# Windowed attention with a cosine-gated MLP: casts and weights issued earlier, block loads ahead of outputs, MLP units recounted in four blocks

## The chip, the cores and the metric

One core of a Trainium2 chip runs the kernel. The metric is the device time of one execution in microseconds (us), lower is better. Before the change it is 408.87 us, the median of 3 runs (406.36 to 410.55).

## The reference

Eight batches of eight heads, 576 positions of 64 elements. A query sees keys at a distance of at most 32, and eight global positions see and are seen by everything. The attention's output, laid out as 4608 tokens of 512 elements, goes through an MLP with h·cos(h) between its two products.

```python
scores = scale * np.matmul(q, k.transpose(0, 1, 3, 2))
mask = np.abs(pos[:, None] - pos[None, :]) <= window          # 32
mask = mask | is_global[:, None] | is_global[None, :]
attn = softmax(np.where(mask, scores, -1e9))                  # eight global positions
x = np.matmul(attn, v).transpose(0, 2, 1, 3).reshape(4608, 512)
h = x @ w_in                                                  # 512 x 2048
out = (h * np.cos(h)) @ w_out                                 # 2048 x 512
```

## The kernel before

**Work and its tiles.** Heads are taken in pairs (`pr`, 0 to 31), four pairs to a batch; two pairs make a half batch, and one half batch is one block `s` (0 to 15) of the main loop. For a pair, `scores` (L500 to L503) multiplies keys by queries in three groups of windows (`st`), takes the exponential on ScalarE (`e`) and masks on VectorE (`pm`). `values` (L512 to L523) multiplies by the values (`pv`) and normalises on VectorE (`xn`). `turn_x` (L535 to L543) transposes on TensorE (`tx`) and writes the tokens into `xT`, after a batch's last pair with eight small GpSimd copies for the global positions. The MLP runs on tiles `t` of 512 tokens. An in unit (`mlp_in`, L551 to L555) is four matmuls into `ph`, a cosine on ScalarE and a product on VectorE; 16 of them make `g` of one tile. An out unit (`mlp_out`, L565) is four matmuls into `po`; after four of them `po` is copied out (by VectorE and ScalarE in turn) and SP stores it (L574). There are 144 units of each kind.

**Inputs.** For half batches 0 to 3 keys and queries are loaded by GpSimd (`load_qk`), transposed on TensorE (`turned`) and copied by ScalarE and VectorE (`local_k`, `local_q`). Values come by 24 loads on SP (`load_vn`) into `vn32`, are cast by VectorE and ScalarE (`cast_vn`, L343 to L346), and `spread` (L365 to L372) moves them with matmuls into the value tiles `vw` of one pair. From half batch 4 on, `cast_half` has GpSimd's queue cast v, k and q from DRAM to DRAM (`v16`, `k16`, `q16`), and SP then brings them in: `turn_half` (two transposing DMAs into `kT` and `qT`, two buffers each) and `load_values` (into `vw`, four buffers). VectorE copies `kT` and `qT` into `kw` and `qb` (L477, L490).

**The order.** It is written by hand. `FRONT` is a list of steps for the first six pairs: `k1` is `local_k(1)`, `C0` is `cast_vn(0)`, `w0` is `spread(0)`, `s1.0` the first group of scores of pair 1, `p` is `values`, `x` is `turn_x`, `W` loads a quarter of `w_in`, `O` loads `w_out`, `V` is `hold`, `n` is `x_squares`, a checksum on ScalarE, and `I` loads the positions into GpSimd's registers. A `hold` is a GpSimd copy of one element of `vn32`, which keeps what follows in GpSimd's queue until that load has landed. The blocks 2 and 3 have lists of their own, `THIRD` and `FOURTH`; all later ones use `ORDER`. In these `1` is an in unit and `2` an out unit, and the letter behind a step names a pair: `a` and `z` are the block's own two, `c` and `d` the next block's. `G` runs `casts(s)`: a copy that waits for the block's `xn` (the gate), the casts of a later half batch, and in block 4 also six indirect loads of the global rows of batches 4 to 7 (`gather`), which `build_globals(1)` uses at the end of block 5. In units run only for tiles whose tokens are there (`ready`), out units up to the cap `outs_by`. At the end of a block SP is given the loads of the block after next. Blocks 4 and 5 take half batches 4 and 5, which are the fifth and the sixth.

Of the kernel before, what the change touches and what calls it, by code (L numbers as in the profile page):

```python
# [23 lines left out]
G = 8  # L24
# [17 lines left out]

THIRD = "1 1 C2 w4 pa 1 w5 1 xa V3 W3 O pz kc qc 1 1 xz kd qd 1 C3 wc G 1 wd n 1 1"

FOURTH = "sa0 sa1 sa2 sz0 sz1 sz2 pa 1 1 xa pz 1 1 G xz n R 2 1 2 1 2 1 2 1 2 1 2 1 2 1 2 kc qc 1 2 1 2 kd qd 1 2 1 2"

FRONT = ("s0.0 s0.1 s0.2 k1 q1 C0 w0 s1.0 s1.1 s1.2 L2 p0 k2 q2 C1 w1 x0 s2.0 s2.1 s2.2 p1 g4 k3 q3 w2 W1 x1 s3.0 s3.1 s3.2 p2 L3 g5 w3 x2 k4 q4 p3 "
         "g6 g7 I s4.0 s4.1 s4.2 x3 n0 k5 q5 V2 W2 s5.0 s5.1 s5.2")
OK_ALL = float(P * (B * NP * 2 * BP + B))
# [144 lines left out]
def kernel(  # L194
# [462 lines left out]

    def load_w_out(_):
        nc.gpsimd.dma_start(w_out16, moe_w_out.rearrange("(c p) n -> p c n", p=P))
        cast_half(4, "vkq")  # L660

    STEPS = {"s": scores, "p": values, "x": turn_x}
    with tc.manual_schedule():
# [40 lines left out]
        def load_values(pr):  # L704
            load_v(pr)
            load_vg(pr)
# [9 lines left out]
        def globals_kq(pr):  # L716
            globals_k(pr)
            globals_q(pr)

        def casts(s):  # L720

            nc.gpsimd.tensor_copy(gate, xn_of[s][0:1, 1, 0, 0:1])  # L722
            for n in range(4, 2 * B):
                if s == n - 3:
                    cast_half(n, "vkq")
            if s == 4:
                for src, dst in ((k, kg32), (q, qg32), (v, vg32)):
                    gather(src, dst, 1)

        LOCAL = {"k": local_k, "q": local_q}  # L730
        OTHER = LOCAL | {"g": globals_kq, "L": load_qk, "W": load_w_in, "c": lambda s: cast_half(s, "v"), "v": load_values, "n": x_squares,
                 "I": load_idx, "w": spread, "C": cast_vn, "V": hold, "O": load_w_out}
        for step in FRONT.split():
# [9 lines left out]
        for s in range(2, B * NP // 2):  # L743
            outs_by[0] = 16 if s < 5 else 8 * (s - 3)
            for pr in (2 * s + 2, 2 * s + 3):
                if 8 <= pr < B * NP:
                    globals_kq(pr)
            for step in {2: THIRD, 3: FOURTH}.get(s, ORDER).split():
# [6 lines left out]
                elif step == "R":  # L755
                    ready[0] = 2
                elif step == "G":
                    casts(s)
# [6 lines left out]
            if s % 2 == 1:  # L765
                ready[0] = s // 2 + 1 + (s // 2 == B - 1)
            if s < B * NP // 2 - 2:
                turn_half(s + 2)
                load_values(2 * s + 4)
                load_values(2 * s + 5)  # L770
            if s == 5:
# [50 lines left out]
```

## Time and profile before

| what | value |
|---|---|
| median of 3 runs | 408.87 us (406.36 to 410.55) |
| the profiled execution's own time | 405.1 us |
| its span, first to last instruction | 403.4 us |
| mean granted TensorE clock | 0.954 |
| TensorE matmul busy | 348.2 us, 86% |
| VectorE busy | 266.5 us, 66% |
| ScalarE busy | 249.6 us, 62% |
| GpSimd busy | 111.1 us, 28% |

The busy times are of one profiled execution; its span is 1.7 us shorter than its time. A busy share is a mean over stages with different limits, so it is the single blocks that have to be looked at: block 2 runs from 50.30 to 81.34 us, block 3 to 115.72, block 4 to 133.11, block 5 to 146.72, block 6 to 165.84. After block 15, near 315 us, only MLP units are left.

### The profile page before, as it was taken

What the parts mean: (1) busy time and instruction counts of PE and PEld (TensorE: products, weight loads), DVE (VectorE), ACT (ScalarE), POOL (GpSimd) and SP (SyncE); (2) the same over time, 40 slices, a digit from 0 to 9 for tenths busy, and PEclk for the clock granted to TensorE, in tenths of its full rate; (3) what the DMA queues carried; (4) which work ended last, traced back from release to release, by engine and by line L of the source; (5) the groups of instructions that cost most, each with busy time, mean ns of one, the idle gap of its engine ahead of it and who ended that gap; (6) DMA issues with size and microseconds to landing.
All of it is one profiled execution on the core that took longest, in us unless ns stands there. A gap on an engine that the chain in (4) does not pass through costs nothing.

```text
span 403.4 us, 7909 instructions
## 1 busy us (share of the span) xinstructions
PE 348.2 (86%) x2934; PEld 191.7 (48%) x2934; DVE 266.5 (66%) x615; ACT 249.6 (62%) x372; POOL 111.1 (28%) x249
## 2 busy tenths in 40 slices
PE   0499579777998459999999999999999969999993
PEld 0388446543444335555555555555555424444441
DVE  7649457455557857788887888878888445544300
ACT  5567646484458626768777786777867866244300
POOL 6734352306003644442516416141100100000000
PEclk9999579889999859999999999999999999999998
DMA  6996099999339999999999999999980000010111
GB/s 100 198 208 93 4 181 196 158 84 75 57 77 118 178 117 150 187 122 199 106 172 161 141 193 143 177 170 128 160 81 34 26 2 26 26 54 27 54 78 59
DMA packets 175318, 45.55 MB, mean 113 GB/s; under 512 B 163881, under 2 KB 170281, under 8 KB 175081
## 3 DMA queue, kind: packets, MB, share of 16 engines
q1 hardware_dynamic: 111449, 27.41, 50.4%
q0 software_dynamic: 63824, 17.57, 44.1%
q8 instruction: 25, 0.41, 0.4%
q14 instruction: 20, 0.16, 0.2%
HBM read 45.07 MB, written 20.05 MB: 161 GB/s over the span
## 4 chain that ended last, share of the span: by engine, by line
PE 71%; DVE 8%; ACT 7%; DMA 5%; issue 4%; POOL 4%; POOLq 0%; ACTq 0%; DVEq 0%
PE po L565 29%; PE ph L551 26%; PE st L500 5%; PE t L369 4%; DVE g L555 4%; PE pv L512 3%; DMA vg<-in_v_dram,gidx_rows 3%; ACT cos L554 2%; PE tx L535 2%; PE t L365 2%; DMA kn<-in_k_dram 2%; ACT e L502 2%; POOL q L257 1%; ACT qb L487 1%; DVE qb L487 1%
## 5 line engine op out<-in xcount | busy, mean ns | idle before, releaser
L551 PE MATMUL ph<-xT,w_in 128*128 128x512 f16 x576 | 143.8, 385 | 7.0 <-DVE g L555 5.0
L554 ACT ACTIVATE cos<-ph,pio 128x512 f16<-128x512 f32 x144 | 97.2, 686 | 74.7 <-PE ph L551 72.3
L565 PE MATMUL po<-w_out,g 128*128 128x512 f16 x576 | 142.1, 383 | 1.1 <-DVE o L572 1.1
L555 DVE TENSOR_TENSOR g<-cos,ph 128x512 f16<-128x512 f16 x144 | 96.4, 686 | 66.2 <-ACT cos L554 62.8
L551 PEld LDWEIGHTS <-w_in 128*128 128x128 f16 x576 | 54.1, 99 | 69.2 <-issue 12.4
L565 PEld LDWEIGHTS <-g 128*128 128x128 f16 x576 | 55.8, 98 | 65.2 <-issue 3.7
L502 ACT ACTIVATE e<-st 128x512 f16<-128x512 f32 (+1 forms) x96 | 47.7, 563 | 15.4 <-PE st L500 10.0
L503 DVE TENSOR_TENSOR pm<-e,mask 128x512 f16<-128x512 f16 (+1 forms) x96 | 37.3, 404 | 25.3 <-ACT e L502 23.3
L722 POOL COPY gate<-xn 1x1 f16<-1x1 f16 x14 | 2.5, 179 | 162.4 <-DVE xn L523 162.4
L500 PE MATMUL st<-qb,kw 128*128 128x128 f16 x352 | 30.3, 233 | 13.1 <-DVE qb L487 4.9
L500 PEld LDWEIGHTS <-kw 128*128 128x128 f16 x352 | 25.4, 104 | 22.6 <-issue 11.6
L523 DVE TENSOR_TENSOR xn<-pv,r_all 128x768 f16<-128x768 f32 x32 | 30.6, 958 | 1.9
L369 PE MATMUL t<-xT 112*128 112x128 f16 (+1 forms) x168 | 23.0, 255 | 5.7 <-DVE xT L343 5.2
L257 POOL DMA_DIRECT2D q<-in_q_dram x12 | 26.2, 2183 | 0.0
L570 ACT COPY o<-po 128x512 f32<-128x512 f32 x18 | 10.5, 585 | 22.4 <-PE po L565 22.1
L543 POOL COPY xT<-xg 128x4 f16 x64 | 19.7, 308 | 14.8 <-DVE xT L538 11.4
L584 ACT ACTIVATE sq<-xn 128x1536 f16<-128x1536 f16 x16 | 23.6, 1478 | 0.0
L535 PE MATMUL tx<-ident,xn 128*128 128x128 f16 x192 | 17.0, 228 | 6.6 <-DVE xn L523 6.6
L490 DVE COPY qb<-qT 64x616 f16<-64x616 f16 x48 | 22.1, 460 | 0.3
L535 PEld LDWEIGHTS <-xn 128*128 128x128 f16 x192 | 13.4, 102 | 14.7 <-DVE xn L523 9.1
L572 DVE COPY o<-po 128x512 f32<-128x512 f32 x18 | 12.3, 684 | 12.0 <-PE po L565 12.0
L365 PE MATMUL t<-vg,xT 128*128 128x128 f16 x88 | 20.2, 255 | 0.0
(121 smaller groups left out, 342.5 us busy)
## 6 DMA issues: line engine op xcount, KB each, us to landing
out_dram<-o SPq DMA_DIRECT2D x36, 256.0 KB
vw<-v SPq DMA_DIRECT2D x35, 165.0 KB
v<-in_v_dram POOLq DMA_DIRECT2D x12, 288.0 KB, 5.1
k<-in_k_dram POOLq DMA_DIRECT2D x12, 288.0 KB, 8.0
q<-in_q_dram POOLq DMA_DIRECT2D x12, 288.0 KB, 11.8
vn<-in_v_dram SPq DMA_DIRECT2D x20, 112.0 KB
w_in<-in_moe_w_in_dram POOLq DMA_DIRECT2D x4, 512.0 KB, 8.0
w_out<-in_moe_w_out_dram POOLq DMA_DIRECT2D x1, 2048.0 KB, 17.6
```

The source lines that it names most:

```text
L257: nc.gpsimd.dma_start(dst[s].rearrange("t (h d) -> t h d", h=4), dview(src, base, (D, S), (S * D, 4), (1, D)))
L365: nc.tensor.matmul(t[:, j - g0], own[:, pr], vg16[:, 0].rearrange("p h d -> p (h d)"), start=True, stop=False)
L369: nc.tensor.matmul(t[:, j - g0], shift[0:m, a], new[0:m, x, h0 : h0 + 2 * D], start=False, stop=(a, x) == parts[-1])
L500: nc.tensor.matmul(st[:, j], kp[:, g0 + j], view(qp[:, g0 + j], (1, P)), start=True, stop=True)
L502: nc.scalar.activation(e[:, :n], st[:, :n], AF.Exp, scale=scale)
L503: nc.vector.tensor_tensor(view(pm[:, g0], (1, n * P)), view(e, (1, n * P)), view(mask[:, g0], (1, n * P)), ALU.mult)
L523: nc.vector.tensor_tensor(view(xn, (384, 2), (D, 6), (1, D)), view(pv, (512, 2), (65, 6), (1, D)), view(rp, (6, 2), (1, 6), (0, D)), ALU.mult)
L535: nc.tensor.transpose(tx[:, n], xn[:, n], ident16)
L551: nc.tensor.matmul(ph, w_in16[:, j, f * P : (f + 1) * P], xT[:, j, t * TT : (t + 1) * TT], start=(j == 0), stop=(j == NC - 1))
L554: nc.scalar.activation(cos, ph, AF.Sin, bias=pio2)
L555: nc.vector.tensor_tensor(g16[:, f], cos, ph, ALU.mult)
L565: nc.tensor.matmul(po, g16[:, f, s * P : (s + 1) * P], w_out16[:, f], start=(f == 0), stop=(f == NF - 1))
```

## The change

It moves steps and changes counts; apart from the two holds, and from a few table loads that ScalarE needs where cosines and exponentials now alternate, the same instructions run. The holds `V2` and `V3` go. `W2` moves up to behind `W1`; `W3` and `O` move from block 2 and the end of `FRONT` to a place before pair 3's `turn_x`; `O` now issues the cast of half batch 4's values ahead of `w_out`, and the new step `K` issues its keys and queries and all of half batch 5. The casts of half batches 6 and 7 move one block earlier (`G` of blocks 2 and 3), so `G` of block 4 has only the gathers. `C2` moves from block 2 into `FRONT`, `n0` the other way, `C3` from right before `wc` to one unit before it. For block 5 SP's loads (`bring`) are issued inside block 3 (step `T`), ahead of that block's outputs; for block 4 the value loads now stand ahead of the transposes. Units: block 2 keeps 10 in units; block 3 goes from 15 in and 12 out to 6 in and 8 out; block 4 from 7 in and 4 out to 8 and 4; block 5 from none to 8 and 4. At the end of block 5 both kernels have run 32 in units and 16 out units.

```diff
-THIRD = "1 1 C2 w4 pa 1 w5 1 xa V3 W3 O pz kc qc 1 1 xz kd qd 1 C3 wc G 1 wd n 1 1"
+THIRD = "1 1 w4 n0 pa 1 w5 1 xa pz kc qc C3 1 wc 1 xz kd qd 1 wd 1 n 1 1 G"
...
-FOURTH = "sa0 sa1 sa2 sz0 sz1 sz2 pa 1 1 xa pz 1 1 G xz n R 2 1 2 1 2 1 2 1 2 1 2 1 2 1 2 kc qc 1 2 1 2 kd qd 1 2 1 2"
+FOURTH = "sa0 sa1 sa2 sz0 sz1 sz2 pa 1 1 xa pz G 1 1 xz T n R 1 1 2 2 2 2 kc qc 2 2 kd qd 2 2"
...
-FRONT = ("s0.0 s0.1 s0.2 k1 q1 C0 w0 s1.0 s1.1 s1.2 L2 p0 k2 q2 C1 w1 x0 s2.0 s2.1 s2.2 p1 g4 k3 q3 w2 W1 x1 s3.0 s3.1 s3.2 p2 L3 g5 w3 x2 k4 q4 p3 "
-         "g6 g7 I s4.0 s4.1 s4.2 x3 n0 k5 q5 V2 W2 s5.0 s5.1 s5.2")
+FRONT = ("s0.0 s0.1 s0.2 k1 q1 C0 w0 s1.0 s1.1 s1.2 L2 p0 k2 q2 C1 w1 x0 s2.0 s2.1 s2.2 p1 g4 k3 q3 w2 W1 W2 x1 s3.0 s3.1 s3.2 p2 L3 g5 w3 x2 C2 p3 "
+         "g6 g7 I W3 O k4 x3 K q4 s4.0 s4.1 s4.2 k5 q5 s5.0 s5.1 s5.2")
...
     def load_w_out(_):
+        cast_half(4, "v")
         nc.gpsimd.dma_start(w_out16, moe_w_out.rearrange("(c p) n -> p c n", p=P))
-        cast_half(4, "vkq")
+
+    def cast_more(_):
+        cast_half(4, "kq")
+        cast_half(5, "vkq")
...
+        def bring(s):
+
+            if s > 4:
+                turn_half(s)
+            load_values(2 * s)
+            load_values(2 * s + 1)
+            if s == 4:
+                turn_half(s)
...
-            for n in range(4, 2 * B):
-                if s == n - 3:
+            for n in range(6, 2 * B):
+                if s == n - (4 if n < 8 else 3):
                     cast_half(n, "vkq")
...
-            outs_by[0] = 16 if s < 5 else 8 * (s - 3)
+            outs_by[0] = 4 * (s - 1) if s < 5 else 8 * (s - 3)
...
+                elif step == "T":
+                    bring(s + 2)
...
-            if s < B * NP // 2 - 2:
-                turn_half(s + 2)
-                load_values(2 * s + 4)
-                load_values(2 * s + 5)
+            if s != 3 and s < B * NP // 2 - 2:
+                bring(s + 2)
```

On ScalarE the cosine of each in unit stands in a row of L554, so the recount can be read there. From the first cosines of block 3 to the first exponentials of block 4 it was, before:

```order
L554 ACTIVATE cos<-ph,pio_71 128x512 x4
L584 ACTIVATE sq,x_sq<-xn 128x1536
L554 ACTIVATE cos<-ph,pio_71 128x512 x7
L570 COPY o<-po 128x512
L554 ACTIVATE cos<-ph,pio_71 128x512 x4
L502 ACT_TABLE_LOAD
L502 ACTIVATE e<-st 128x512 x2
```

and it is now:

```order
L554 ACTIVATE cos<-ph,pio_71 128x512 x4
L584 ACTIVATE sq,x_sq<-xn 128x1536
L554 ACTIVATE cos<-ph,pio_71 128x512 x2
L570 COPY o<-po 128x512
L502 ACT_TABLE_LOAD
L502 ACTIVATE e<-st 128x512 x2
```

Nine of the fifteen cosines have left block 3, and the copy of an output stands last before the table load.

On VectorE in `FRONT`, around the normalising of pair 3 (`xn`, L523), the two casts of `cast_vn(2)` (L343, L346) come in, and the copy of pair 4's queries (`qb`, L487) goes behind pair 3's `turn_x`. Before:

```order
L538 COPY xT_82<-tx_773 128x616
L487 COPY qb0_99<-t_800 64x11x56
L517 TENSOR_REDUCE dg_841<-pv_292 8x2
L518 RECIPROCAL r_all_119<-pv_292 128x12
L519 RECIPROCAL r_all_119<-dg_841 8x12
L523 TENSOR_TENSOR xn_728<-pv_292,r_all_119 128x768
L503 TENSOR_TENSOR pm_932<-e_938,mask_114 128x512
```

and now:

```order
L538 COPY xT_82<-tx_774 128x616
L343 CAST xT_82<-vn32_112 112x768
L346 CAST xT_82<-vn32_112 16x256
L517 TENSOR_REDUCE dg_808<-pv_292 8x2
L518 RECIPROCAL r_all_119<-pv_292 128x12
L519 RECIPROCAL r_all_119<-dg_808 8x12
L523 TENSOR_TENSOR xn_729<-pv_292,r_all_119 128x768
L537 TENSOR_REDUCE xg_529<-tx_920 128x8
L538 COPY xT_82<-tx_920 128x616
L487 COPY qb0_99<-t_942 64x11x56
```

The scores of pair 4 need that `qb`, so they now follow pair 3's normalising and turning.

On GpSimd at the gate of block 4, ahead of the globals' copies for block 6 (`kw0`, `qb0`), stood before:

```order
L722 COPY gate_113<-xn_1901 1x1
L253 DMA v16_81<-in_v_dram 16x9216
L257 DMA k16_80<-in_k_dram 2304x1x64
L257 DMA q16_79<-in_q_dram 2304x1x64
L293 DMA kg32_104<-in_k_dram,gidx_rows_106 128x64 x2
L293 DMA qg32_103<-in_q_dram,gidx_rows_106 128x64 x2
L293 DMA vg32_105<-in_v_dram,gidx_rows_106 128x64 x2
L454 COPY kw0_95<-kgT_116 128x11x8
```

and now:

```order
L735 COPY gate_113<-xn_1809 1x1
L293 DMA kg32_104<-in_k_dram,gidx_rows_106 128x64 x2
L293 DMA qg32_103<-in_q_dram,gidx_rows_106 128x64 x2
L293 DMA vg32_105<-in_v_dram,gidx_rows_106 128x64 x2
L454 COPY kw0_95<-kgT_116 128x11x8
```

The cast of half batch 7 has gone from in front of the gathers to the gate of block 3.

## Rows read from the trace of the kernel before

**Rows 1.** Windows, blocks 2 to 7: us, busy per engine, clock, DMA share, GB/s
```profile
50.30:81.34 31.04, 25.46 (x291) 17.50 (x290) 17.19 (x40) 17.22 (x27) 10.96 (x15) 0.86 1.51 177
81.34:115.72 34.38, 29.02 (x187) 13.79 (x186) 20.00 (x41) 19.31 (x30) 6.88 (x18) 0.95 0.68 64
115.72:133.11 17.39, 13.60 (x123) 6.94 (x122) 12.60 (x30) 12.71 (x20) 4.94 (x5) 1.00 1.04 129
133.11:146.72 13.61, 5.12 (x81) 3.89 (x81) 10.78 (x28) 6.57 (x14) 5.59 (x9) 0.66 1.52 138
146.72:165.84 19.12, 19.12 (x143) 9.96 (x143) 12.39 (x29) 10.98 (x17) 13.54 (x31) 0.88 1.46 154
165.84:182.75 16.91, 16.91 (x143) 9.06 (x142) 14.54 (x34) 12.92 (x19) 5.47 (x12) 1.00 1.51 152
```
**Rows 2.** Timeline of TensorE, blocks 3 and 4: start, us, operation, [idle <-releaser]
```profile
93.83 1.03 PE L565 MATMUL po<-w_out,g 128*128 128x512 f16 x4
94.70 1.03 PE L551 MATMUL ph<-xT,w_in 128*128 128x512 f16 x4
...
99.60 1.02 PE L551 MATMUL ph<-xT,w_in 128*128 128x512 f16 x4 [1.28 <-POOL xT L543]
...
117.13 2.75 PE L565 MATMUL po<-w_out,g 128*128 128x512 f16 x12 [0.62 <-DVE o L572]
...
133.11 0.77 PE L500 MATMUL st<-qb,kw 128*128 128x128 f16 x11 [1.18 <-issue]
```
**Rows 3.** Timeline of TensorE, block 2: spreads of pairs 4 to 6
```profile
55.92 0.27 PE L369 MATMUL t<-xT 112*128 112x128 f16 x1 [2.70 <-DVE xT L343]
...
59.58 0.45 PE L512 MATMUL pv<-vw,pm 128*64 128x65 f16 x16
...
61.31 0.22 PE L365 MATMUL t<-vg,xT 128*128 128x128 f16 x1
...
63.55 1.03 PE L551 MATMUL ph<-xT,w_in 128*128 128x512 f16 x4
...
72.91 0.27 PE L369 MATMUL t<-xT 112*128 112x128 f16 x1 [2.25 <-DVE xT L343]
```
**Rows 4.** Timeline of VectorE, end of the front and block 2
```profile
39.84 0.47 DVE L538 COPY xT<-tx 128x616 f16<-128x616 f16 x1
42.00 0.80 DVE L487 COPY qb<-t 64x616 f16<-64x616 f16 x1 [1.69 <-ACT qb L487]
...
43.42 0.96 DVE L523 TENSOR_TENSOR xn<-pv,r_all 128x768 f16<-128x768 f32 x1
...
54.55 1.31 DVE L343 CAST xT<-vn 112x768 f16<-112x768 f32 x1
...
72.30 0.55 DVE L343 CAST xT<-vn 112x768 f16<-112x768 f32 x1
```
**Rows 5.** Timeline of TensorE, end of the front: scores of pairs 4 and 5
```profile
42.95 1.33 PE L500 MATMUL st<-qb,kw 128*128 128x128 f16 x11 [2.18 <-DVE qb L487]
...
49.17 1.33 PE L500 MATMUL st<-qb,kw 128*128 128x128 f16 x11 [2.68 <-DVE qb L487]
```
**Rows 6.** Timeline of ScalarE, end of the front: the checksum of block 0
```profile
44.91 1.49 ACT L584 ACTIVATE sq<-xn 128x1536 f16<-128x1536 f16 x1
```
**Rows 7.** Timeline of GpSimd: a hold, block 4's gate, block 6's globals
```profile
49.63 0.18 POOL L336 CAST gate<-vn 1x1 f16<-1x1 f32 x1
...
127.80 0.18 POOL L722 COPY gate<-xn 1x1 f16<-1x1 f16 x1 [26.75 <-DVE xn L523]
...
146.41 0.26 POOL L459 COPY qb<-qgT 64x88 f16<-64x88 f16 x1 [6.44 <-DMA vg<-in_v_dram,gidx_rows]
```
**Rows 8.** Timeline of SP's queue: block 3's outputs, then block 5's keys
```profile
102.75 14.68 SPq L574 DMA_DIRECT2D out_dram<-o  x3
117.53 1.34 SPq L269 DMA_TRANSPOSE kT<-k  x1
```
**Rows 9.** A window in the front, in the columns of rows 1
```profile
32.00:34.00 2.00, 2.00 (x66) 1.95 (x61) 1.93 (x6) 1.68 (x3) 1.17 (x2) 1.00 0.05 9
```

More of the change, by code (lines that the diff above doesn't have):

```diff
@@ L731 @@
         OTHER = LOCAL | {"g": globals_kq, "L": load_qk, "W": load_w_in, "c": lambda s: cast_half(s, "v"), "v": load_values, "n": x_squares,
-                 "I": load_idx, "w": spread, "C": cast_vn, "V": hold, "O": load_w_out}
+                 "I": load_idx, "w": spread, "C": cast_vn, "V": hold, "O": load_w_out, "K": cast_more}
         for step in FRONT.split():
```

## The prediction

> **What bounds the kernel now.** I read the windows first. The reader is to see that a block with the full load of 8 in units and 8 out units, block 7, takes 16.91 us, and that TensorE is busy for all of it [rows 1]: from block 6 on the matmuls are the limit, and nothing that comes earlier can make these blocks shorter. The four blocks ahead are different: block 2 takes 31.04, block 3 34.38, block 4 17.39 and block 5 13.61 us, and TensorE is busy for 25.46, 29.02, 13.60 and 5.12 of these [rows 1]. So 96.42 us hold some 23 us without matmuls, and in block 5 alone 8.5. Block 5 runs no MLP unit, because its cap and the tokens that are ready leave it none, while block 3 has 27 of the 48 units of these blocks.
>
> Second I read TensorE's timeline, for what a unit costs and what TensorE waits for. Back to back an out unit starts at 93.83 and the in unit behind it at 94.70 [rows 2]: 0.865 us a unit, or 23.4 of block 3's 34.38 us. Block 2 stands still twice, for 2.70 and 2.25 us, before a spread whose cast on VectorE is not done [rows 3].
>
> Third the clock. After each such wait it falls: the means of blocks 2 and 5 are 0.86 and 0.66, block 6 begins in it (0.88), and blocks 4 and 7 have 1.00 [rows 1]. At 1.2 GHz the spread of pair 4 takes 59.58 - 55.92 = 3.66 us, that of pair 5 at 2.4 GHz 63.55 - 61.31 = 2.24 us [rows 3].
>
> Last the queues. GpSimd's gate of block 4 comes at 127.80, behind it the casts of half batch 7 and then the gathers, and a copy for block 6 waits 6.44 us until the last has landed, to 146.41 [rows 7]. SP's transposes for block 5 start at 117.53, behind block 3's outputs, which were waited for from 102.75 [rows 8].
>
> **The change part by part.** Times are against the profiled execution.
>
> *The front.* The queries of pair 4 now come behind the casts of C2 and the normalising and turning of pair 3. Before, `xT` ended at 40.31, the normalising at 44.38, and the scores began at 42.95 [rows 4, 5]. Now the chain is: 40.31; the casts, 1.31 for the large one and some 0.3 for the small; the normalising with its reciprocals, as before from the end of `qb` at 42.80 to 44.38, 1.58; two short transposing steps at the low clock, estimated at 1.3, the copies of ScalarE, 0.7, and VectorE's `qb`, 0.80. That ends at 46.3, 3.4 us later than before. Then the checksum of 1.49 us [rows 6] no longer stands in front of pair 5's copies, so the scores of pair 5 are 1.9 us later. For the cast the rows give 1.31 at 54.55 and 0.55 at 72.30 [rows 4]; the shorter one makes it 1.1. I take +1.5, bounds 0 and +2.5.
>
> The Trainium skill (GPSIMD Engine Reference, Specifications) says that GpSimd's SBUF interfaces are shared with VectorE. The cast of 1.31 us fell into GpSimd's issue of casts and would bear that out. By that rule C2, now beside the issue of `W3` and `O`, takes the long time, and the front's term is +1.9 in place of +1.5.
>
> *Holds.* They cost 0.18 us of GpSimd, off every chain [rows 7]. What goes with them is the order of transfers. `W2` now transfers in the front. DMA was free at 32 to 34 us, share 0.05 [rows 9], so it fills a gap: cost 0, and 1 us at most if the blocks of v that C2 casts at 40.3 come behind it. The first MLP unit waits for pair 3's global copies, which now stand behind `W3` and `O` on GpSimd: `W3`, a cast and `w_out` are three issues while VectorE is still on pair 3, hidden. If that cover is gone the in units are late by the rest of them, an estimate of 1 us; both ends are in the front's bounds.
>
> The Trainium skill (DMA: Bandwidth & Descriptors, Issuing engines are not separate DMA queues) says that transfers of all issuing engines run on the same DMA engines and interleave, which speaks against dropping holds. By the rows the gap is there; by the rule alone I would add that 1 us to the sum.
>
> *C2 out of block 2.* The wait of 2.70 goes, and with it the slow clock of that spread, 3.66 - 2.24 = 1.4: -4.1. Next to be late there is nothing of DMA but ScalarE, which gains the checksum; it is busy for 17.22 of 31.04 us [rows 1], so 0, at most +1.5. C3 still follows pair 6's copies and has one unit (0.865 us) in front of the spread, as before: its 2.25 us stay. Bounds of the part -6 and -2.
>
> *Units out of block 3.* 13 units less, 13 x 0.865 = 11.25 us, all on TensorE's path. With them goes the 1.28 us for which a unit of tile 1 waits for GpSimd's global copies [rows 2]. Together -12.5; bounds -13 and -10.
>
> *Block 4.* It had 11 units in 17.39 us, with waits for VectorE and ScalarE, from 0.62 at 117.13 to 1.18 at 133.11 [rows 2]. The eighth in unit fits into the last. The copy of an output on ScalarE now precedes the table load: +0.5. Bounds -3 and +1.
>
> *Block 5.* From none to 12 units, the load of block 4. So it takes block 4's 17.39 us, and then the two transposes of the globals, which before stood in an idle block. Each needs a cast and a copy on ScalarE behind the last cosine: a cosine, two casts, a copy and two transposes, about 2.0 us, an estimate. That makes 19.4, or +5.8 against 13.61. The gathers now start at the gate, without 4 us of casts in front of them, and a whole block before they are needed: their wait goes. Bounds +2.5 and +10.4; the latter is 12 x 0.865, with nothing hidden.
>
> *SP's queue.* Block 5's loads no longer wait for outputs. Outputs are behind 10 load issues instead; three output buffers and only three outputs until block 5 hide that. Casts of 6 and 7 one block earlier: the block-3 window has a DMA share of 0.68 [rows 1]. Cost 0, at most +2.
>
> *Block 6.* It began at the low clock and took 19.12 in place of 16.91. With block 5 filled as block 4 is, whose clock was 1.00, that goes: -2.2; bounds -2.2 and 0.
>
> Sum: +1.5 - 4.1 - 12.5 + 0.5 + 5.8 - 2.2 = -11.0 us. Blocks 7 to 15 and the tail keep their work and their 16.91 us, so nothing gives it back. The profiled 405.1 becomes 394.1. The median of the runs is 3.8 above the profiled time; I take the difference off the median: 408.87 - 11.0 = 397.9 us.
>
> **The rivals.**
>
> *Units in block 5 do not hide.* Its 13.61 us were a chain of VectorE, busy for 10.78 [rows 1]; if the units come on top of it the block takes 13.61 + 10.4 = 24.0, 4.6 more than I said. For it: TensorE idles there for VectorE's results. Against: block 4, with 11 units and 12.60 us of VectorE, did the same work in 17.39. Time 402.5.
>
> *Blocks 4 and 5 run like block 7 without four units.* 16.91 - 4 x 0.865 = 13.45 each, 3.9 less than I took, because their inputs are there earlier: 397.9 - 7.8 = 390.1. For it: block 7 has no waits. Against: block 4's waits are for VectorE and ScalarE, not for loads, and out units are what hides these in block 7.
>
> *Slower: the clock stays low from block 3's second half on.* These blocks are thinner in matmuls than before. If the clock falls in block 3 and does not rise until block 6, ten units there, and 24 units and the attention in blocks 4 and 5, run at 1.2 GHz. The ratio of the two spreads is 3.66 / 2.24 = 1.63, so a unit costs 0.545 more: 34 x 0.545 = 18.5, and the attention's matmuls (13.60 - 9.5 = 4.1 us a block) 2 x 2.6 = 5.2. Block 4's idle time is 3.8 us a block and takes up 7.6 of these; block 6's 2.2 come back. Net +18.3, time 416. It decides from the point where block 4 loses the 2.4 GHz in more than half of it. For it: blocks 2 and 5. Against: block 4 had 1.00 with 11 units.
>
> *No gain.* The time saved turns into waits for transfers: with blocks 3 to 5 some 10 us shorter, the casts and transposes of blocks 6 to 8 would be late, with block 7 at a DMA share of 1.51 [rows 1]. Against: casts 6 and 7 were issued a block earlier, and TensorE waits for nothing in block 7, busy for all its 16.91 us [rows 1]. Time 407 to 410.
>
> **How the numbers follow.** Chances: the forecast, 394 to 401, 0.55; units on top 0.18; shorter blocks 0.13; no gain 0.08; slower by the clock 0.06. A measurement of this kernel tells about 1%, 4 us, from no change, so faster means below 404.8: 0.55 + 0.13 and nearly all of 0.18, 0.85. Within 1%: the case of no gain and the rest, 0.09; slower 0.06. The range goes from between the shorter blocks and the forecast, 391, to the upper end of the units on top, 405.
>
> **What would show it.** Right: no wait of 2.7 us at pair 4's spread; block 3 at 21 to 23 us; block 4 near 17.9 and block 5 near 19 us, with a clock near 1.0; block 6 starting near 136 and taking 16.9 us; no wait of GpSimd for the gathers into block 6. Wrong: block 5 at 22 us or more, a granted clock below 0.8 in blocks 3 to 5, a wait of `kw` or `qb` for a transpose, or a front that is late by more than 3 us.

## The result and the profile after

| | before | after |
|---|---|---|
| median of the runs (4 each) | 407.62 us | 393.08 us |
| lowest and highest | 405.76, 410.55 | 391.96, 393.95 |
| profiled execution | 405.1 us | 393.95 us |
| its span | 403.4 us | 392.1 us |

The ratio of the two is 0.9635, with a 95% interval from 0.9566 to 0.9705: faster. The prediction was 397.9 us in a range from 391 to 405. The profiled executions differ by 11.15 us, and the sum of the steps was 11.0; the medians differ by 14.5 us. (With a fourth run the median of before is 407.62; the prediction started from 408.87.)

The windows of the kernel after, cut at the same work as those of [rows 1]: blocks 2 to 7, each from its first matmul (block 2 from the first MLP unit) to the next block's. Columns as there.

```profile
51.61:81.65 30.04, 25.66 (x291) 16.28 (x290) 18.44 (x38) 18.95 (x30) 9.11 (x14) 0.83 1.75 166
81.65:103.35 21.70, 17.78 (x136) 8.84 (x135) 14.68 (x33) 11.97 (x18) 7.00 (x18) 0.92 1.25 130
103.35:119.90 16.55, 14.46 (x128) 7.35 (x127) 11.90 (x29) 12.62 (x19) 3.77 (x5) 1.00 0.82 100
119.90:138.03 18.13, 14.62 (x129) 7.48 (x130) 15.34 (x35) 13.99 (x23) 10.18 (x23) 1.00 1.14 125
138.03:154.95 16.92, 16.92 (x143) 9.11 (x143) 13.69 (x32) 12.74 (x20) 6.73 (x16) 1.00 0.93 87
154.95:171.87 16.92, 16.92 (x143) 9.08 (x142) 14.55 (x34) 12.92 (x19) 5.45 (x11) 1.00 1.35 144
```

Beside [rows 1] the reader sees where the time went, as a small table (after less before, and what the prediction gave):

| stretch | before | after | difference | forecast |
|---|---|---|---|---|
| to the first unit | 50.30 | 51.61 | +1.3 | +1.5 |
| block 2 | 31.04 | 30.04 | -1.0 | -4.1 |
| block 3 | 34.38 | 21.70 | -12.7 | -12.5 |
| block 4 | 17.39 | 16.55 | -0.8 | +0.5 |
| block 5 | 13.61 | 18.13 | +4.5 | +5.8 |
| block 6 | 19.12 | 16.92 | -2.2 | -2.2 |

One row stands out: block 2 gave 3.1 us less than the forecast, and blocks 4 and 5 gave 2.6 us more. TensorE's timeline of block 2 after, to be set beside [rows 3], shows that the wait of 2.70 us at pair 4's spread is gone, that the other is still there, and that a new one stands behind it:

```profile
67.33 0.22 PE L369 MATMUL t<-xT 112*128 112x128 f16 x1 [2.42 <-DVE xT L343]
...
70.20 0.26 PE L369 MATMUL t<-xT 16*128 16x128 f16 x1 [1.13 <-DVE xT L346]
...
70.90 1.91 PE L551 MATMUL ph<-xT,w_in 128*128 128x512 f16 x4
```

The second wait is for the small cast of C3, 16 rows of 256 elements. VectorE's timeline of the same stretch:

```profile
66.72 0.56 DVE L343 CAST xT<-vn 112x768 f16<-112x768 f32 x1
67.19 2.95 DVE L346 CAST xT<-vn 16x256 f16<-16x256 f32 x1
70.18 0.69 DVE L555 TENSOR_TENSOR g<-cos,ph 128x512 f16<-128x512 f16 x1
```

And GpSimd's, where the gate of block 2 now lets half batch 6's casts out:

```profile
65.92 0.18 POOL L735 COPY gate<-xn 1x1 f16<-1x1 f16 x1 [10.60 <-DVE xn L523]
66.16 0.51 POOL L253 DMA_DIRECT2D v<-in_v_dram  x1
66.66 1.76 POOL L257 DMA_DIRECT2D k<-in_k_dram  x1
67.98 2.05 POOL L257 DMA_DIRECT2D q<-in_q_dram  x1
```

The small cast took 0.27 us for half batch 2 in the same execution (at 40.63). Here it ends at 70.14, 0.11 us behind the end of GpSimd's last issue at 70.03. The kernel before has an issue behind the same gate, half batch 5's, but C3 stood behind its end there: the large cast began at 72.30 [rows 4], the small one at 72.77.

```profile
70.13 2.19 POOL L257 DMA_DIRECT2D q<-in_q_dram  x1
...
72.77 0.33 DVE L346 CAST xT<-vn 16x256 f16<-16x256 f32 x1
```

So the change did two things here: it put half batch 6's issue where half batch 5's had been, and it moved C3, with its spread `wc`, forward into it, past three units, pair 5's turn and pair 7's copies. Its large cast now starts 66.72 - 65.92 = 0.8 us behind the gate; in the kernel before it was 72.30 - 68.12 = 4.2 us. (C3 at its old distance from the gate was not run.) The theory after the result was: **half batch 6's casts, moved a block ahead, hold VectorE at C3, and that took most of C2's gain back**. The rival was that C2's wait had been worth less than 4.1 us from the start, because TensorE waits at C3 anyway. A second question was why blocks 4 and 5 hide the units so well, and what each part of the change is worth alone.

### The profile page after: what moved, and what is told of

It reads as the page before. It is cut to its first block, busy times and chain, and to the rows that moved or that the text cites. A ratio compares the mean times of both kernels' runs of the same rounds, so it can differ in the third digit from the quotient of the medians.

```text
span 392.1 us, 7906 instructions
## 1 busy us (share of the span) xinstructions
PE 345.4 (88%) x2934; PEld 188.7 (48%) x2934; DVE 268.1 (68%) x615; ACT 252.4 (64%) x374; POOL 111.5 (28%) x247
## 4 chain that ended last, share of the span: by engine, by line
PE 77%; DVE 7%; ACT 7%; issue 4%; DMA 3%; POOL 1%; POOLq 0%; ACTq 0%; DVEq 0%
PE po L565 31%; PE ph L551 30%; PE st L500 5%; PE pv L512 3%; PE t L369 3%; PE tx L535 3%; ACT cos L554 2%; DVE g L555 2%; ACT e L502 2%; DMA kn<-in_k_dram 2%; DVE xn L523 1%; DMA vg<-in_v_dram,gidx_rows 1%; PE t L365 1%; ACT sq L584 1%; DVE xT L346 1%
## 5 line engine op out<-in xcount | busy, mean ns | idle before, releaser
L554 ACT ACTIVATE cos<-ph,pio 128x512 f16<-128x512 f32 x144 | 97.3, 687 | 66.3 <-PE ph L551 66.1
L565 PE MATMUL po<-w_out,g 128*128 128x512 f16 x576 | 139.0, 379 | 0.8 <-DVE o L572 0.8
L523 DVE TENSOR_TENSOR xn<-pv,r_all 128x768 f16<-128x768 f32 x32 | 30.7, 958 | 2.5 <-ACT sq L584 0.6
L570 ACT COPY o<-po 128x512 f32<-128x512 f32 x18 | 10.6, 586 | 29.4 <-PE po L565 28.9
L257 POOL DMA_DIRECT2D q<-in_q_dram x12 | 27.0, 2250 | 0.0
L369 PE MATMUL t<-xT 112*128 112x128 f16 (+1 forms) x168 | 20.2, 233 | 4.3 <-DVE xT L343 2.7
L490 DVE COPY qb<-qT 64x616 f16<-64x616 f16 x48 | 22.1, 460 | 0.3
L257 POOL DMA_DIRECT2D k<-in_k_dram x12 | 20.8, 1734 | 0.5 <-issue 0.5
```

The source lines that it names most:

```text
L257: nc.gpsimd.dma_start(dst[s].rearrange("t (h d) -> t h d", h=4), dview(src, base, (D, S), (S * D, 4), (1, D)))
L369: nc.tensor.matmul(t[:, j - g0], shift[0:m, a], new[0:m, x, h0 : h0 + 2 * D], start=False, stop=(a, x) == parts[-1])
L523: nc.vector.tensor_tensor(view(xn, (384, 2), (D, 6), (1, D)), view(pv, (512, 2), (65, 6), (1, D)), view(rp, (6, 2), (1, 6), (0, D)), ALU.mult)
L554: nc.scalar.activation(cos, ph, AF.Sin, bias=pio2)
L565: nc.tensor.matmul(po, g16[:, f, s * P : (s + 1) * P], w_out16[:, f], start=(f == 0), stop=(f == NF - 1))
```

## The experiments

All are compared with the kernel before on the same chip, whose medians there were 407.9 to 410.2 us. They ran on four chips: recount_alone, no_recount, c3_early and casts_late on one; gathers_early, recount_gathers, late_bring and holds_back on a second; cast6_late and c2_back on a third; after_again and c2_back2 on a fourth. Between runs of different groups a difference of 1 or 2 us is not clear of the chips' own. In the diffs a - is the changed kernel's line (of recount_alone and recount_gathers: the kernel before's).

**recount_alone.** The kernel before with the new units of block 3 and the new cap alone.

```diff
-FOURTH = "... xa pz 1 1 G xz n R 2 1 2 1 2 1 2 1 2 1 2 1 2 1 2 kc qc 1 2 1 2 kd qd 1 2 1 2"
+FOURTH = "... xa pz 1 1 G xz n R 1 1 2 2 2 2 kc qc 2 2 kd qd 2 2"
-            outs_by[0] = 16 if s < 5 else 8 * (s - 3)
+            outs_by[0] = 4 * (s - 1) if s < 5 else 8 * (s - 3)
```

> The kernel before with only the new unit counts of blocks 3 to 5. Theory A (the recount is the gain: 13 units leave a block that TensorE fills and go into two that it does not): block 3 near 22 us, block 4 near 16.5, block 5 near 18 to 20, block 2 unchanged at 31; 393 to 397 us. Rival B (the earlier casts and gathers are the gain; without them block 6 waits for the gathers behind the casts of half batch 7, and block 5 for its transposes behind outputs): the gathers land after block 6 is due, a wait of some 5 us into block 6 or at block 5, 400 us or more.

Measured: 400.17 us, ratio 0.9812 [0.9743, 0.9881]; 8.2 us of the gain, where 393 to 397 us were expected. Its windows of blocks 3 to 5:

```profile
82.64:104.96 22.32, 17.80 (x135) 8.74 (x134) 14.70 (x33) 12.56 (x20) 7.00 (x18) 0.92 1.14 88
104.96:121.52 16.56, 14.46 (x128) 7.34 (x127) 11.90 (x29) 12.62 (x19) 4.95 (x5) 1.00 1.15 130
121.52:143.74 22.22, 16.43 (x128) 8.25 (x129) 15.59 (x35) 13.87 (x23) 12.74 (x26) 0.92 1.58 129
```

Block 3 falls by 12.1 us, so the price of a unit, 0.865 us, was right. Block 5 takes 22.2 us, though, 4.1 more than in the changed kernel with the same units, and past the 18 to 20 expected. Its wait for the gathers (7.32 us on GpSimd) ends at 135.88, ahead of block 6, so the rival's mechanism is not there, though its 400 us or more is.

**no_recount.** The changed kernel with the old units and the old cap (the same two lines turned round).

> The changed kernel with the old unit counts of blocks 3 to 5. Theory A: blocks 3 to 5 take their old 34, 17 and 12 to 13.6 us, block 5 idle as before; what is left is the wait for the gathers at block 6 and its low clock, 404 to 408 us. Rival B: most of the gain stays, below 399 us.

Measured: 407.04 us, ratio 0.9963 [0.9927, 0.9999]. All that is not the new count is worth 1.3 us by itself, and with the count 7.1 us (400.17 - 393.08), of which 4.1 are in block 5. Block 5, with no unit in it, took 16.60 us here, not the 12 to 13.6 expected, and block 6 opened with a wait and at a low clock:

```profile
131.75:148.35 16.60, 5.17 (x81) 3.82 (x81) 12.34 (x26) 6.47 (x14) 9.14 (x18) 0.63 1.37 115
```

```profile
148.35 1.33 PE L500 MATMUL st<-qb,kw 128*128 128x128 f16 x11 [3.86 <-POOL xT L543]
```

```profile
148.35:167.55 19.20, 19.20 (x143) 10.08 (x144) 13.68 (x32) 10.99 (x17) 8.03 (x20) 0.88 0.77 70
```

The trace puts that wait down to GpSimd's `xT`. But VectorE's copies of `kw` and `qb`, which these scores also need, end at 148.24, 0.11 us ahead of them, and the copy of `kw` took 3.31 us where it takes 0.53 elsewhere. It stands beside GpSimd's issue of half batch 8:

```profile
144.08 3.31 DVE L477 COPY kw<-kT 128x1320 f16<-128x1320 f16 x1
147.31 0.93 DVE L490 COPY qb<-qT 64x616 f16<-64x616 f16 x2
```

```profile
144.84 2.19 POOL L257 DMA_DIRECT2D q<-in_q_dram  x1
```

So the 12 units that the changed kernel has in block 5 cost it 18.13 - 16.60 = 1.5 us against this kernel, whose block 5 has a delay of its own, and 4.5 us against the kernel before. They bring back 2.3 us of block 6's clock.

**c3_early.** C3 (the casts of half batch 3) stands right behind C2's old place, ahead of half batch 6's issue.

```diff
-THIRD = "1 1 w4 n0 pa 1 w5 1 xa pz kc qc C3 1 wc ..."
+THIRD = "1 1 w4 n0 C3 pa 1 w5 1 xa pz kc qc 1 wc ..."
```

> The changed kernel with cast_vn(3) moved up to before pair 4's values, where VectorE is idle and GpSimd issues nothing. Theory A (the small cast took 2.95 us in place of 0.27 because GpSimd was issuing the casts of half batch 6; the spread of pair 6 waited 2.42 and 1.13 us for it, and the clock fell): both casts take 0.6 and 0.3 us, no wait at that spread, clock up, block 2 falls from 30.0 to 25 to 27 us; 387 to 390 us. Rival C (ScalarE or the copies of pair 6 are next in line and block 2 does not shorten): 392 us or more.

Measured: 388.32 us, ratio 0.9503 [0.9436, 0.957]. It beats both kernels. Its window of block 2, and its small cast:

```profile
52.56:77.53 24.97, 23.56 (x291) 15.16 (x290) 15.81 (x38) 18.62 (x30) 8.99 (x14) 0.92 1.73 174
```

```profile
58.72 0.28 DVE L346 CAST xT<-vn 16x256 f16<-16x256 f32 x1
...
66.90 0.80 DVE L487 COPY qb<-t 64x616 f16<-64x616 f16 x1
67.73 0.69 DVE L555 TENSOR_TENSOR g<-cos,ph 128x512 f16<-128x512 f16 x1
68.34 0.69 DVE L372 CAST vw<-t 128x512 f16<-128x512 f32 x1
```

GpSimd issues half batch 6 from 67.17 to 70.93 in this run. Three other operations of VectorE now stand beside that issue and have the length that they have elsewhere. So the issue does not hold VectorE as such, but some of its operations; the last section says which. This version also takes away TensorE's wait of 2.42 us for C3's large cast, so its gain is more than the hold's price.

**casts_late.** Half batches 6 and 7 are issued a block later again, as before the change.

```diff
-                if s == n - (4 if n < 8 else 3):
+                if s == n - 3:
```

> The changed kernel with the casts of half batches 6 and 7 at their old gates, in blocks 3 and 4. Theory A: nothing waits for these casts; the small cast of block 2 is short again because GpSimd's issue is gone from beside it, block 2 1 to 3 us shorter, and the gathers, now behind the cast of half batch 7, land just before block 6 needs them: 390 to 393 us. Rival B: the gathers come late again and block 6 waits, 395 us or more.

Measured: 394.73 us, ratio 0.9685 [0.9614, 0.9755], where 390 to 393 us were expected. The first theory holds in block 2: the cast takes 0.34 us and the block 26.82, which is the forecast's -4.1 against before (31.04 - 26.82 = 4.2). The time does not fall, because block 5 is 3.9 us longer than in the changed kernel. In block 5 TensorE and ScalarE stand still without a releaser that the trace names (`issue`: nothing that it shows was waited for; `remote`: an event that it puts down to no instruction):

```profile
50.67:77.49 26.82, 23.55 (x290) 15.18 (x289) 15.97 (x38) 18.78 (x30) 6.30 (x13) 0.93 1.56 170
...
115.74:137.79 22.05, 15.05 (x129) 7.80 (x130) 15.29 (x35) 13.87 (x23) 12.42 (x26) 1.00 1.29 136
```

```profile
122.16 0.24 PE L512 MATMUL pv<-vw,pm 128*64 128x65 f16 x3 [1.19 <-issue]
...
123.60 0.28 PE L512 MATMUL pv<-vw,pm 128*64 128x65 f16 x5 [1.20 <-issue]
...
123.65 0.60 ACT L502 ACTIVATE e<-st 128x512 f16<-128x512 f32 x1 [4.72 <-remote]
```

From 116 to 120 us the packets of the software queue alone took 197.1% of the sixteen engines' time (a sum over packets, which passes 100% where they overlap). On GpSimd half batch 7's casts (from 110.68) and six gathers (114.73 to 122.09) are issued one behind the other; recount_alone has the same pair at 116.45 to 128.1.

**gathers_early.** casts_late, with the gathers for the second batch put behind block 3's gate.

```diff
-            if s == 4:
+            if s == 3:
                 for src, dst in ((k, kg32), (q, qg32), (v, vg32)):
                     gather(src, dst, 1)
```

> casts_late (half batch 6's cast behind block 3's gate, 7's behind block 4's) with the six gathers moved ahead from block 4's gate to block 3's, behind half batch 6's cast. Theory (block 5's stalls of 1.19 and 1.20 us on TensorE and 4.72 us on ScalarE come where half batch 7's cast and the gathers keep the DMA engines full together): block 5 falls from 22.05 us to between 18 and 19.5, the rows without a visible releaser are gone, and the time is 390.5 to 392 us. Rival (half batch 7's cast alone, a block later than in the changed kernel, is what jams block 5): block 5 stays at 21 us or more, the time at 394 or above. Second rival: the stall moves with the gathers into block 4, which then takes 19 us or more against 16.6, and the time stays at 393 to 395.

Measured: 390.81 us, ratio 0.9564 [0.9512, 0.9616], 3.9 us under casts_late. Block 5 is back at its length:

```profile
117.91:136.04 18.13, 14.62 (x128) 7.47 (x129) 15.18 (x36) 13.68 (x23) 6.56 (x17) 1.00 1.44 150
```

Half batch 7's casts are where casts_late had them; the gathers alone were moved. The changed kernel, with the gathers behind block 4's gate and these casts a block earlier, has no stall either. So it is the two together that jam block 5. That they do it by filling the DMA engines is not shown: the software queue's share is the same here, in the first four microseconds of a block 5 without the stall, as in casts_late (below: casts_late from 116 to 120 us, then gathers_early from 118 to 122).

```profile
q0 software_dynamic: 3880, 0.50, 197.1%
...
q0 software_dynamic: 3900, 0.50, 196.0%
```

**recount_gathers.** recount_alone with the same edit.

> The kernel before with the new counts of MLP units in block 3 (recount_alone, 400.17 us) and the six gathers moved ahead from block 4's gate to block 3's, behind half batch 6's cast. Theory (half batch 7's cast and the gathers together jam block 5, which took 22.2 us in recount_alone): block 5 falls to between 18 and 19.5 us and the time to 396 to 397.5 us. Rival (the cast alone jams it, or the late block loads do): block 5 stays above 21 us and the time at 399 to 401.

Measured: 395.71 us, ratio 0.9672 [0.9608, 0.9736], 4.5 us under recount_alone, and again 18.13 us in block 5:

```profile
123.23:141.36 18.13, 14.62 (x129) 7.47 (x129) 15.17 (x36) 13.68 (x23) 6.61 (x16) 1.00 1.72 147
```

With the new count and this one number the kernel before comes within 2.6 us of the changed one.

**late_bring.** Block 5's loads back at the end of block 3, behind its outputs on SP's queue.

```diff
-FOURTH = "... xa pz G 1 1 xz T n R ..."
+FOURTH = "... xa pz G 1 1 xz n R ..."
-            if s != 3 and s < B * NP // 2 - 2:
+            if s < B * NP // 2 - 2:
```

> The changed kernel with block 5's loads (its transposed turns and its values) back behind block 3's last unit, so behind the outputs that block 3 puts on SyncE's queue; everything else as changed. Theory of the prediction (SP's queue order is worth nothing, at most 2 us): 393 us within 1, block 5 within 0.5 us of its 18.1, and no TensorE wait in block 5 that a DMA ends. Rival (the loads ahead of the outputs are what let blocks 3 to 5 run without waits): block 4 or block 5 opens with a DMA wait of 2 us or more on TensorE or ScalarE and the time is 395 us or above.

Measured: 394.11 us, ratio 0.9645 [0.9592, 0.9698]; 1.0 us above the changed kernel's 393.08. Block 5 takes 19.80 us, and ScalarE waits in it as in casts_late, only shorter:

```profile
118.21:138.01 19.80, 15.09 (x128) 7.44 (x129) 15.41 (x35) 13.88 (x23) 9.86 (x23) 1.00 1.40 147
```

```profile
121.25 0.60 ACT L502 ACTIVATE e<-st 128x512 f16<-128x512 f32 x1 [1.33 <-remote]
```

Block 5 is 1.7 us longer, which is more than the 0.5 of the expectation, but no DMA wait of TensorE stands there either, so the rival's mechanism does not show. In this profile SP's order is worth 1.7 us of block 5: inside the prediction's bound of 2, though not its value of 0. In the time it is not clear of the noise (ratio 0.9645 against 0.9635).

**holds_back.** Holds again ahead of the weights of chunks 2 and 3.

```diff
-... w2 W1 W2 x1 ... I W3 O k4 ...
+... w2 W1 V2 W2 x1 ... I V3 W3 O k4 ...
```

> The changed kernel with the two holds put back on GpSimd ahead of the weight loads of chunks two and three (each a copy that waits for a load of its half batches), at the places where these loads stand now. Theory of the prediction (the holds cost the path nothing): 393 us within 1, the first unit within 0.3 us of 51.6. Rival (a hold keeps GpSimd from issuing the weights and the casts of half batches four and five in time): the first unit or block 2 is later by 1 us or more, TensorE or SyncE waits for a cast, and the time is 394.5 us or above.

Measured: 393.75 us, ratio 0.9645 [0.9589, 0.9701], and the first unit at 50.99 us, 0.6 earlier than in the changed kernel, where 0.3 either way was expected. The holds cost nothing that shows.

**cast6_late.** Of the two casts only half batch 6's is moved back, to part the two effects of casts_late.

```diff
-                if s == n - (4 if n < 8 else 3):
+                if s == n - (4 if n == 7 else 3):
```

> The changed kernel with only half batch 6's cast moved back a block (from block 2's gate to block 3's); half batch 7's cast stays behind block 3's gate and the gathers behind block 4's. Theory (half batch 6's issue on GpSimd is what holds VectorE's small cast of C3 for 2.95 us, and half batch 7's cast beside the gathers is what jammed block 5 in casts_late): the small cast takes 0.3 us, block 2 takes 26.8 us, block 5 18.1 to 18.5, and the time is 389 to 391 us. Rival (casts 6 and 7 behind one gate in block 3 fill the DMA engines there): block 3 or 4 is longer by 2 us or more, and the time stays at 392 to 395.

Measured: 391.01 us, ratio 0.9537 [0.9492, 0.9582]. The small cast takes 0.34 us and block 5 18.50:

```profile
66.54 0.34 DVE L346 CAST xT<-vn 16x256 f16<-16x256 f32 x1
```

```profile
51.26:79.17 27.91, 24.57 (x291) 15.54 (x290) 15.88 (x38) 18.73 (x30) 6.31 (x13) 0.89 1.58 167
```

```profile
116.34:134.84 18.50, 14.62 (x128) 7.46 (x129) 15.35 (x35) 13.89 (x23) 10.19 (x23) 1.00 1.18 128
```

Block 2 was expected at 26.8 and took 27.9 with a lower clock; the rest came as the theory said. Half batch 6's issue holds the cast; half batch 7's, beside the gathers, jams block 5.

**c2_back.** The changed kernel with C2 in block 2 again.

```diff
-FRONT = "... w3 x2 C2 p3 ..."
+FRONT = "... w3 x2 p3 ..."
-THIRD = "1 1 w4 n0 ..."
+THIRD = "1 1 C2 w4 n0 ..."
```

> The changed kernel with C2 (the casts of half batch 2's values on VectorE) back in block 2, behind its first two MLP units; everything else as changed, with half batch 6's cast still issued in block 2. Theory of the prediction (C2 stands for 4.1 us of block 2, of which the collision at C3 took back 2.95): block 2 is 2 to 4 us longer than the changed kernel's 30.0, with a wait of some 2.7 us on TensorE at pair 4's spread, the front is no more than 1.5 us shorter, and the time is 395 to 397 us. Rival (TensorE's wait at C2 only takes the place of its wait at C3, so that C2 is worth nothing while C3 is held): block 2 within 1 us of 30.0 and the time 392 to 394 us.

Measured: 396.03 us, ratio 0.9648 [0.9596, 0.97]. In microseconds it is 2.95 above the changed kernel (2.3 without its longest run, 400.8 us), but the kernel before was slower on that chip as well, and by the ratio the two hardly differ. Its profiled execution is that longest run, so nothing is read from it. It was run again beside the changed kernel, on one chip.

**after_again and c2_back2.** The changed kernel unedited, and c2_back.

> The changed kernel once more, unedited, as the neighbour of c2_back2 on one chip (c2_back stood 2.95 us above the changed kernel in microseconds, but its neighbour before was slower too, so that the ratios hardly differ). Expected by both theories: 392 to 395 us, a ratio of 0.960 to 0.966, block 2 at 29.5 to 30.1 us.

> c2_back once more, beside the changed kernel (C2 back in block 2, all else as changed). Theory (TensorE's wait at pair 4's spread, 1.86 us in c2_back, comes on top of the held cast at C3): 2 to 4 us above after_again in the medians, block 2 at 32 to 34 us in its profile. Rival (C2's place is worth nothing while C3 is held): within 1 us of after_again, block 2 within 1 us of its 30.0; c2_back's profiled 35.4 us was then an outlier by its clock of 0.69.

Measured: 392.23 us for the changed kernel (391.54 to 392.46), ratio 0.965 [0.9597, 0.9703], and 395.64 for C2 in block 2 (393.44 to 398.69), ratio 0.9745 [0.9682, 0.9807]: 3.4 us. The expectation for c2_back2's time held; those for block 2 missed in both: 31.27 us where 32 to 34 were expected, and 28.03 where 29.5 to 30.1 were. The windows of block 2, of after_again first:

```profile
51.72:79.75 28.03, 23.61 (x291) 15.17 (x290) 18.49 (x38) 18.78 (x30) 9.12 (x14) 0.93 1.77 171
```

```profile
49.59:80.86 31.27, 25.44 (x290) 17.31 (x289) 19.60 (x40) 19.18 (x31) 11.18 (x16) 0.87 1.71 166
```

C2 in block 2 costs 3.2 us there and gives 2.1 back in the front of this pair; the two profiled executions differ by 1.4 us, the medians by the 3.4. The ranges of the runs do not overlap, so C2's move is worth something while C3 is held, and the rival falls. The theory's way of adding up is not what the profile shows: the spread behind C3 runs mostly at 1.2 GHz in c2_back2 (granted clock 0.55 from 68.44 to 72.01), and TensorE does not wait for the held cast in it.

The same two kernels, the changed one and its repetition, also show what the hold costs. In both the small cast takes 2.95 us and TensorE waits 1.13 and 1.16 us for it, behind the same 2.42 us for the large one. Block 2 takes 30.04 us in one and 28.03 in the other. Windows of 2 us behind the hold, of the first profile and then of after_again, tell them apart by the granted clock (the number behind POOL's):

```profile
70.00:72.00 2.00, 1.80 (x7) 0.74 (x7) 1.44 (x3) 0.48 (x1) 1.46 (x7) 0.50 2.09 144
72.00:74.00 2.00, 2.00 (x26) 1.34 (x26) 0.42 (x1) 0.69 (x1) 0.00 (x0) 0.50 1.70 200
74.00:76.00 2.00, 2.00 (x26) 1.06 (x22) 0.77 (x3) 1.78 (x2) 0.00 (x0) 0.57 1.68 130
```

```profile
70.00:72.00 2.00, 1.64 (x13) 0.89 (x13) 1.60 (x3) 0.52 (x2) 1.63 (x7) 1.00 2.38 219
72.00:74.00 2.00, 2.00 (x43) 1.13 (x41) 1.19 (x3) 1.92 (x3) 0.00 (x0) 1.00 1.34 120
```

In the first the clock falls to 0.50, which is 1.2 GHz; in the second it stays at 2.4 GHz. Why it falls in one and not in the other is not shown. The low clock is the usual case: late_bring, holds_back and no_recount have the held cast as well. Their block 2, and then that of gathers_early, without the hold:

```profile
50.49:79.98 29.49, 25.45 (x291) 16.32 (x289) 18.39 (x38) 18.86 (x30) 9.88 (x16) 0.84 1.70 164
50.99:80.93 29.94, 25.64 (x291) 16.23 (x290) 18.39 (x38) 18.89 (x30) 9.14 (x14) 0.83 1.74 168
51.20:80.68 29.48, 25.45 (x290) 16.37 (x289) 18.39 (x38) 18.87 (x30) 9.93 (x16) 0.84 1.70 168
...
52.53:79.35 26.82, 23.55 (x291) 15.17 (x289) 15.96 (x38) 18.79 (x30) 5.53 (x11) 0.93 1.51 169
```

The five profiles with the hold have a mean of 29.4 us; the three without it (26.82 twice, and 27.91 in cast6_late) one of 27.2. So the hold costs some 2.2 us of block 2: 1.2 where the clock is the same (28.03 against 26.82 at 0.93), and up to 3.2 where it falls. cast6_late, at 0.89, shows that it can fall there without the hold too.

## Why the prediction was right, and where its sum was not

That the sum of -11.0 meets the profiled -11.15 is luck: C2's term came out 3.1 us short, and blocks 4 and 5 took 2.6 us less than forecast. The median, 393.08, lies in the range, but 0.9 below the band from 394 to 401 that carried the chance of 0.55. Of the signs of being right, block 3 (21.70), the clock of blocks 4 and 5 (1.00), block 6 (16.92) and the missing wait at pair 4's spread came as said, and GpSimd's wait for the gathers, 2.65 us, ends at 126.38, in block 5. Block 6 starts at 138.03; "near 136" does not follow from the prediction's own steps, which give 146.72 - 8.8 = 137.9.

*Units out of block 3: -12.5, measured -12.7* in the changed kernel and -12.1 alone. Counting units at the 0.865 us of the timeline was enough, because block 3's units stood on TensorE's path with nothing beside them.

*Block 5: +5.8, measured +4.5; block 4: +0.5, measured -0.8.* The mechanism, units fill waits for VectorE and ScalarE, was right; block 4 was the model for block 5, and both came out 1.3 us shorter than their figure. The rival "units in block 5 do not hide" is out: it wanted 10.4 us for the 12 units, and they cost 4.5 us against the kernel before and 1.5 against no_recount. Both blocks kept a clock of 1.00, so the slower rival, which wanted 1.2 GHz in blocks 4 and 5, is out too. The rival of shorter blocks wanted 13.45 us each; they took 16.55 and 18.13, with TensorE busy for 14.46 and 14.62. Its price was wrong besides: against the 17.9 and 19.4 us of the forecast it is 10.4 us less, not 7.8, so 387.5 us, not 390.1. No gain is out as well: block 6 takes 16.92 us and waits for nothing. The price depends on what else is in block 5, which the prediction did not see: with half batch 7's casts and the gathers issued together, the block took 22.1 and 22.2 us, its mark for "wrong". The changed kernel keeps them apart; the prediction counted that as a shorter wait of the gathers, not as this.

*Block 6: -2.2, measured -2.2*, and no_recount, without units in block 5, kept the low clock of 0.88 in block 6 (19.20 us). That is the prediction's reason, tested.

*C2 out of block 2: -4.1, measured -1.0.* This term failed in the sum, outside its bounds of -6 and -2, but not by its own mechanism: without the hold, in casts_late, gathers_early and cast6_late, block 2 took 26.82, 26.82 and 27.91 us, 3.1 to 4.2 less than before. (Other small moves are in that difference; C2 alone, put back with the hold in place, costs 3.2, and without the hold it was not put back.) **The step that was wrong is "Casts of 6 and 7 one block earlier: the block-3 window has a DMA share of 0.68 [rows 1]. Cost 0, at most +2."** It looked at these casts as transfers, and at a DMA share. Half batch 6's issue on GpSimd holds VectorE's small cast for 2.95 us at C3, where before the cast took 0.33 us, and block 2 paid some 2.2 us for it, clock included. Half batch 7's earlier issue saves more than that: with it late, block 5 takes 22.05 us (casts_late) in place of 18.50 (cast6_late). So the casts together cost nothing in the time, as the step said (393.08 us against 394.73 with both late), but as the difference of two effects that it did not see. The prediction had the row that hinted at the first, C2's large cast of 1.31 against 0.55 [rows 4], and used it for the front only.

*The front: +1.5, measured +1.3* in the profiled pair. This is weaker than it looks. The first unit stood between 50.49 and 52.56 us in nine profiles with the new front, with a mean of 51.45, and between 50.30 and 51.51 in three with the old one, with a mean of 50.82. By the means the front costs 0.6 us.

The Trainium skill (GPSIMD Engine Reference, Specifications) says that GpSimd shares its SBUF interfaces with VectorE, with contention for VectorE's instructions in a 2-port performance mode or with two SBUF inputs. The prediction weighed the sharing for C2 in the front, where it did not apply: there the casts took 0.55 and 0.27 us, at 40.16 and 40.63, ahead of GpSimd's issues from 42.77. At C3 the trace agrees that VectorE can be held, 2.95 against 0.34 us; it does not show the mode of an instruction. Two SBUF inputs alone do not do it here: the three `pm`, which read `e` and `mask` from SBUF, took 1.23 us together at 51.74, beside GpSimd's issue of q (51.51 to 54.73), and 1.24 at 36.36 without an issue.

*The holds: 0, measured 0.7 us or less*, within the scatter. *SP's queue: 0, measured 1.7 in block 5* of one profile, and in the time no more than the scatter.

*From the profile to the median.* The prediction took 11.0 off the median of before, 408.87, which lay 3.8 us above its profiled execution, and so came out 4.8 us too high. The changed kernel's profiled execution does not lie below its median: it is 0.9 above it. Beside after_again the kernel before scattered over 403.9 to 410.7 us, the changed kernel over 391.5 to 392.5. The offset belonged to before and should not have been carried over whole; with the profiled time alone, 394.1, the forecast would have been 1.0 off.

## What to carry to other kernels

A DMA that is moved to an earlier place is priced twice: as a transfer, and as an issue on the engine that starts it, beside whatever stands there on the neighbouring engines; look at both timelines over the same microseconds. A filling of one block with another's work pays by the waits that it covers, so ask first whether those waits are still there, and what else is due in that block. Compare a step with its own cleanest version: block 2's term, -1.0 in the changed kernel, was -3.1 to -4.2 with half batch 6's issue out of C3's way. And ask what a step collides with before it is kept: c3_early, one word moved in a list, is 3.9 to 4.8 us under the changed kernel's two medians (on other chips), by the hold and by C3's own wait together.

## What the hardware showed that was not expected

The held cast is oddly constant. It took 2.95 us in after_again, late_bring, holds_back, no_recount (2.96) and c2_back2 (2.96), at either clock of TensorE, and ended 0.11 us behind GpSimd's last issue. It is not the only one. In block 5 of the changed kernel a copy of `kw` is held as well, beside half batch 8's issue:

```profile
135.01 0.84 DVE L477 COPY kw<-kT 128x1320 f16<-128x1320 f16 x1
```

```profile
133.30 2.19 POOL L257 DMA_DIRECT2D q<-in_q_dram  x1
```

That copy took 1.55 us in block 3 of cast6_late and 3.31 in no_recount, and in the kernel before C2's cast of 112 rows, the 1.31 us of [rows 4], stood beside this issue:

```profile
53.30 2.18 POOL L257 DMA_DIRECT2D q<-in_q_dram  x1
```

Each of them ends a fixed time behind the end of the issue of q, however early it began: the copies of `kw` 0.36 us in all three, C2's cast 0.38, the 16-row cast 0.11. In the kernel they have in common that they read one tensor in SBUF and write to SBUF. Beside the same issues VectorE's operations that read PSUM (`qb` of L487, `vw`, `xT` of L538) or two tensors (`g`, `pm`) kept their length, and so did copies of `kw` beside the issues of gathers (0.53 us at 118.42). One case does not fit: C3's cast of 112 rows began at 66.72, 0.06 us behind the start of the issue of k, and took its usual 0.56 us. Why it is let through stays open.

The stall in block 5 is open as well. TensorE waited for "issue" (in casts_late and recount_alone) and ScalarE for "remote" (0.87 to 4.72 us in casts_late, recount_alone and late_bring) where the casts of half batch 7 or block 5's loads fell together with the gathers. Instruction loading was a candidate: in casts_late one packet of the instruction queue q8 falls into 123.0 to 123.5 us, just ahead of the end of the stall at 123.6. But its share of the sixteen engines in that half microsecond, 16.6%, makes it 1.3 us long, so it ends behind the stall; and in late_bring it falls into 127.0 to 127.5, long behind the stall's end at 121.25, and in recount_alone into 131.0 to 131.5, behind 129.15. So loading by that queue is not shown to be the cause, nor is a full software queue, which gathers_early has without the stall. That moving the six gathers takes the stall away, twice and by 3.9 and 4.5 us, is shown; by what path they reach ScalarE is not.
